# First chunk of a weight load requested as 120 partitions and 8 partitions

## The chip, the cores and the metric

One core of a Trainium2 chip. The metric is the device time of one execution in microseconds (us). The profile's span is about 1.9 us shorter than that time (80.7 us of span in a run of 82.61 us), and all instants below are counted from the start of the span. Engines: PE is TensorE, PEld its weight loader, DVE VectorE, ACT ScalarE, SP the sync engine that issues nearly all transfers.

## The reference, cut to what matters

A decoding step for one token: layer norm, grouped attention over a window of 4096 cached positions (8 K and V heads, 32 query heads), and beside it a gated feed-forward block; both results are added to the input.

```python
xn = layernorm(x)
out = x + attention(xn, k_cache, v_cache, wq) @ wo + (xn + (silu(xn @ w_gate) * (xn @ w_up)) @ w_down * sigmoid(xn @ w_r))
```

With one row of input there is next to no reuse: each byte of 30.67 MB is read once, and the kernel is a stream of loads with the arithmetic laid beside it. The end of the stream is `wo` (4096 x 512, bf16, 4 MB) and `w_down` (1792 x 512, 1.75 MB).

## The kernel before

Every transfer has its own semaphore. SP issues the whole stream in one order: wq, K cache, V cache, w_gate, w_up, wo in four chunks, w_down in five.

```python
def dma(eng, name, out_, in_):
    s = S("d_" + name)
    eng.dma_start(out=out_, in_=in_).then_inc(s, 16)
    return (s, 16)
...
wo_chunks = [(0, 8), (8, 16), (16, 24), (24, 32)]          # of 32 blocks of 512 columns
t_wo = [dma(sy, f"wo{k}", wo_sb[:, j0 * D:j1 * D], wo_v[:, j0 * D:j1 * D]) for k, (j0, j1) in enumerate(wo_chunks)]
wd_v = B_w_down.rearrange("(p j) n -> p (j n)", j=FB)      # 128 partitions x 14 blocks
wd_chunks = [(0, 4), (4, 8), (8, 11), (11, 13), (13, 14)]
t_wd = [dma(sy, f"wd{k}", wd_sb[:, j0 * D:j1 * D], wd_v[:, j0 * D:j1 * D]) for k, (j0, j1) in enumerate(wd_chunks)]
```

A chunk of wo is 1 MB (8 KB a partition), the first of w_down 512 KB (4 KB a partition). PE takes the chunks in the same order and adds everything up in one PSUM row:

```python
for k, (j0, j1) in enumerate(wo_chunks):
    PE.need(t_wo[k])
    for j in range(j0, j1):
        te.matmul(a_ps, lhsT=oT2[:, j:j + 1], rhs=wo_sb[:, j * D:(j + 1) * D], ...)
PE.need(t_hT)
for k, (j0, j1) in enumerate(wd_chunks):
    PE.need(t_wd[k])
    for j in range(j0, j1):
        ins = te.matmul(a_ps, lhsT=hTr[:, j, 0:1], rhs=wd_sb[:, j * D:(j + 1) * D], ...)
```

Then one DVE addition and the store of 1 KB.

## Time and profile before

| | before |
|---|---|
| time, median (range) | 82.52 us (82.39 to 82.57, 3 runs) |
| span of the profiled run | 80.7 us |
| last landing mark of wo / of w_down | 72.80 / 77.28 us |
| end of the last matmul | 77.81 us |

A *landing mark* is one DMA engine's increment of a transfer's semaphore, as the trace records it. A transfer of 128 rows has sixteen marks in the trace, one for each of the 16 engines, and the sixteenth is what PE waits for: wo's last is at 72.80 us, PE's next matmul starts at 72.84.

### The profile page before, as it was taken

What the parts mean: (1) busy time and instruction counts of PE and PEld (TensorE: products, weight loads), DVE (VectorE), ACT (ScalarE), POOL (GpSimd) and SP (SyncE); (2) the same over time, 40 slices, a digit from 0 to 9 for tenths busy, and PEclk for the clock granted to TensorE, in tenths of its full rate; (3) what the DMA queues carried; (4) which work ended last, traced back from release to release, by engine and by line L of the source; (5) the groups of instructions that cost most, each with busy time, mean ns of one, the idle gap of its engine ahead of it and who ended that gap; (6) DMA issues with size and microseconds to landing.
All of it is one profiled execution on the core that took longest, in us unless ns stands there. A gap on an engine that the chain in (4) does not pass through costs nothing.

```text
span 80.7 us, 1552 instructions
## 1 busy us (share of the span) xinstructions
PE 60.5 (75%) x596; PEld 29.9 (37%) x596; DVE 43.5 (54%) x103; ACT 29.7 (37%) x40; POOL 7.3 (9%) x27
## 2 busy tenths in 40 slices
PE   0012945589999999999988968877888887788950
PEld 0012201386657768667732323222233322123300
DVE  3775000195678977968736678888763380000030
ACT  1941001305696896895860422442222200000000
POOL 5910000101112112121200000000000000000000
PEclk9999999555799999999999999999999999999999
DMA  1899998999999999999999999999999999999400
GB/s 33 309 439 390 455 447 374 434 418 434 418 430 410 434 410 430 414 434 406 430 410 430 406 430 414 445 447 412 426 419 413 418 426 418 416 402 398 138 2 1
DMA packets 4185, 30.72 MB, mean 381 GB/s; under 512 B 467, under 2 KB 598, under 8 KB 1110
## 3 DMA queue, kind: packets, MB, share of 16 engines
q1 hardware_dynamic: 4178, 30.67, 91.7%
q8 instruction: 2, 0.03, 0.2%
q14 instruction: 1, 0.01, 0.0%
q10 hardware_dynamic: 4, 0.00, 0.0%
HBM read 30.67 MB, written 0.00 MB: 380 GB/s over the span
## 4 chain that ended last, share of the span: by engine, by line
SPq 48%; DMA 40%; PE 6%; issue 2%; DVE 1%
SPq L151 48%; DMA k_sb<-in_A_wo_dram 40%; PE ps L467 4%; PE ps L462 2%; DVE res L471 1%; SPq L500 0%; SPq L74 0%
## 5 line engine op out<-in xcount | busy, mean ns | idle before, releaser
L276 ACT COPY kT<-ps 128x1024 bf16<-128x1024 bf16 x19 | 18.5, 1019 | 8.8 <-PE ps L302 8.7
L302 PE MATMUL ps<-ident_bf,kin 128*128 128x128 bf16 x256 | 18.7, 231 | 0.8 <-DVE kin L268 0.6
L302 PEld LDWEIGHTS ps<-ident_bf,kin 128*128 128x128 bf16 x256 | 15.8, 104 | 5.1 <-issue 4.2
L268 DVE COPY kin<-k_sb 128x1024 bf16<-128x1024 bf16 x32 | 12.2, 422 | 0.7 <-PE ps L302 0.7
L273 DVE COPY kT<-ps 128x1024 bf16<-128x1024 bf16 x13 | 9.0, 692 | 4.4 <-PE ps L302 4.3
L462 PE MATMUL ps<-k_sb,oT 128*1 128x512 bf16 x32 | 7.5, 378 | 2.0 <-DMA k_sb<-in_A_wo_dram 2.0
L394 ACT CAST pvS<-ps 128x512 bf16<-128x512 f32 x8 | 4.7, 586 | 9.6 <-PE ps L399 9.6
L471 DVE TENSOR_TENSOR res<-ps,resid 1x512 bf16<-1x512 f32 x1 | 0.7, 679 | 11.5 <-PE ps L467 11.5
L375 DVE COPY vin<-v_sb 128x2048 bf16<-128x2048 bf16 x8 | 5.5, 686 | 1.4 <-PE ps L408 1.4
L381 DVE COPY vin<-v_sb 128x2048 bf16<-128x2048 bf16 x8 | 5.5, 683 | 0.0
L408 PE MATMUL ps<-vin,pTcur 128*16 128x512 bf16 x32 | 3.1, 381 | 2.6 <-ACT pvS L394 2.2
L462 PEld LDWEIGHTS ps<-k_sb,oT 128*1 128x1 bf16 x32 | 2.4, 83 | 7.1 <-DMA k_sb<-in_A_wo_dram 3.2
L420 PE MATMUL ps<-zmov,zst 128*128 128x512 bf16 x16 | 4.7, 377 | 0.0
L228 PE MATMUL ps<-wq_sb,xnT 128*1 128x512 bf16 x32 | 2.9, 499 | 2.3 <-DMA wq_sb<-in_A_wq_dram 2.3
L310 PE MATMUL ps<-kT,qB 128*32 128x512 bf16 x36 | 4.2, 413 | 0.4 <-ACT kT L276 0.3
L244 DVE COPY qpad<-ps 128x16 bf16<-128x16 bf16 x2 | 0.3, 174 | 7.6 <-PE ps L240 7.6
L310 PE MATMUL ps<-kT,qA 128*32 128x512 bf16 x32 | 4.4, 417 | 0.0
L259 POOL COPY qA<-qpad 128x32 bf16<-128x32 bf16 x8 | 2.0, 255 | 20.6 <-DVE qpad L244 10.9
L194 PE MATMUL ps<-ident_bf,xn_row 1*128 1x1 bf16 x4 | 0.3, 165 | 4.6 <-DVE xn_row L189 4.6
L147 PE MATMUL ps<-zmov,zst 128*128 128x512 bf16 x14 | 3.7, 382 | 0.0
L234 ACT CAST q<-ps 128x512 bf16<-128x512 f32 x2 | 1.1, 589 | 6.6 <-PE ps L228 6.6
L414 PE MATMUL ps<-vin,pTcur 128*16 128x512 bf16 x32 | 3.1, 382 | 0.2 <-DVE vin L381 0.2
(85 smaller groups left out, 50.2 us busy)
## 6 DMA issues: line engine op xcount, KB each, us to landing
k_sb<-in_A_k_cache_dram SPq DMA_DIRECT2D x8, 1024.0 KB, 20.6
v_sb<-in_A_v_cache_dram SPq DMA_DIRECT2D x8, 1024.0 KB, 28.2
wq_sb<-in_A_wq_dram SPq DMA_DIRECT2D x2, 2048.0 KB, 9.5
k_sb<-in_A_wo_dram SPq DMA_DIRECT2D x4, 1024.0 KB, 32.0
wq_sb<-in_B_w_gate_dram SPq DMA_DIRECT2D x1, 1792.0 KB, 29.3
wq_sb<-in_B_w_up_dram SPq DMA_DIRECT2D x1, 1792.0 KB, 31.4
k_sb<-in_B_w_down_dram SPq DMA_DIRECT2D x2, 512.0 KB, 31.4
k_sb<-in_B_w_down_dram SPq DMA_DIRECT2D x1, 384.0 KB, 25.7
```

The lines of the kernel that those rows point to most:

```text
L147: te.matmul(ps[:, 7, :], lhsT=zst[:], rhs=zmov[:], start=True, stop=True)
L151: eng.dma_start(out=out_, in_=in_).then_inc(s, 16)
L268: ve.tensor_copy(out=kin[:, b, :], in_=k_sb[:, g, b, :]).then_inc(s_c[b], 1)
L273: ve.tensor_copy(out=kT[:, b, :], in_=tp[:, b, :]).then_inc(s_ev[b], 1)
L276: ac.copy(out=kT[:, b, :], in_=tp[:, b, :]).then_inc(s_ev[b], 1)
L302: ins = te.transpose(tp[:, b, k * P:(k + 1) * P], kin[:, b, k * P:(k + 1) * P], ident_bf[:])
L310: ins = te.matmul(sc[32 * cq:32 * cq + 32, ch, :], lhsT=q[:], rhs=kT[:, b, e * 512:(e + 1) * 512], start=False, stop=False, tile_position= ...
L375: ve.tensor_copy(out=vin[:, 0], in_=v_sb[:, g, 0:16, :]).then_inc(s_va, 1)
L381: ve.tensor_copy(out=vin[:, 1], in_=v_sb[:, g, 16:32, :]).then_inc(s_vb, 1)
L394: ac.copy(out=pvS[:].rearrange("p t d -> p (t d)"), in_=pv_ps).then_inc(s_pvs, 1)
L420: te.matmul(ps[:, 7, :], lhsT=zst[:], rhs=zmov[:], start=True, stop=True)
L462: te.matmul(a_ps, lhsT=oT2[:, j:j + 1], rhs=wo_sb[:, j * D:(j + 1) * D], start=False, stop=False, skip_group_check=True)
```

## The change

Its intent, as far as the words of it tell: 15 engines carry the first chunk of w_down, so the sixteenth has 32 KB less, and what lies behind on its ring (the queue of transfers that one engine works through in order, as the latest engine's marks show: 72.80 us for wo's last chunk, then 74.07, 75.36, 76.30, 76.97 and 77.28 for the five of w_down) lands earlier. The remaining 8 partitions are fetched by a small transfer of their own, one row each on eight engines.

```diff
-    t_wd = [dma(sy, f"wd{k}", wd_sb[:, j0 * D:j1 * D], wd_v[:, j0 * D:j1 * D]) for k, (j0, j1) in enumerate(wd_chunks)]
+    t_wd = []
+    for k, (j0, j1) in enumerate(wd_chunks):
+        rows = [(0, 120), (120, P)] if k == 0 else [(0, P)]
+        t_wd.append([dma(sy, f"wd{k}_{p0}", wd_sb[p0:p1, j0 * D:j1 * D], wd_v[p0:p1, j0 * D:j1 * D]) for p0, p1 in rows])
@@
-        PE.need(t_wd[k])
+        PE.need(*t_wd[k])
```

## The prediction

The traces do not number the engines. The numbers in the prediction are names: 15 for the engine that the 120 rows leave out, 0 to 7 for those that carry a row of the small transfer as well, 8 to 14 for the rest. "Crowding" means that engines slow one another by what they write at the same time. A_wo is wo.

> **What bounds the kernel now.** I read the page first, then the chain that ended last in order of time, then the timeline of the tail, then the transfers of the last microseconds, and at the end the record of single landings in the trace. The page has the 16 DMA engines at 9 tenths or full from slice 3 to the last tenth of the span, and the chain says which transfer counts:
>
> ```profile
> DMA  1899998999999999999999999999999999999400
> GB/s 33 309 439 390 455 447 374 434 418 434 418 430 410 434 410 430 414 434 406 430 410 430 406 430 414 445 447 412 426 419 413 418 426 418 416 402 398 138 2 1
> ...
> q8 instruction: 2, 0.03, 0.2%
> ...
> SPq 48%; DMA 40%; PE 6%; issue 2%; DVE 1%
> ```
>
> ```profile
> 40.85 31.95 DMA k_sb<-in_A_wo_dram
> 72.80 0.04 issue
> 72.84 1.89 PE ps L462 x8
> 74.73 3.10 PE ps L467 x14
> 77.83 0.02 issue
> 77.86 0.68 DVE res L471
> ```
>
> So the chain is: the DMA stream up to the landing of the fourth and last chunk of A_wo (72.80 us), then 22 matmuls on PE without a break (8 on that chunk, 14 on w_down), then one addition and the store. No landing of w_down is in it. That is the point of the whole case, because the change touches w_down alone. The timeline seems to contradict it:
>
> ```profile
> 72.84 1.89 PE L462 MATMUL ps<-k_sb,oT 128*1 128x512 bf16 x8 [0.61 <-DMA k_sb<-in_A_wo_dram]
> 74.35 0.73 PEld L467 LDWEIGHTS ps<-k_sb,hTr 128*1 128x1 bf16 x4
> 74.56 3.25 PE L467 MATMUL ps<-k_sb,hTr 128*1 128x512 bf16 x14
> 75.40 0.55 PEld L467 LDWEIGHTS ps<-k_sb,hTr 128*1 128x1 bf16 x4 [0.32 <-DMA k_sb<-in_B_w_down_dram]
> 76.34 0.30 PEld L467 LDWEIGHTS ps<-k_sb,hTr 128*1 128x1 bf16 x3 [0.40 <-DMA k_sb<-in_B_w_down_dram]
> 77.01 0.09 PEld L467 LDWEIGHTS ps<-k_sb,hTr 128*1 128x1 bf16 x2 [0.36 <-DMA k_sb<-in_B_w_down_dram]
> 77.32 0.08 PEld L467 LDWEIGHTS ps<-k_sb,hTr 128*1 128x1 bf16 x1 [0.23 <-DMA k_sb<-in_B_w_down_dram]
> ```
>
> Four weight loads wait for w_down, 0.32 + 0.40 + 0.36 + 0.23 = 1.31 us. But a weight load runs beside the matmul before it, and the PE row shows its 14 matmuls as one group without a gap. What the waits cost must be read from the starts of the matmuls. Undisturbed, one follows another after 0.215 us (eight of them from 72.84 to 74.56). In the trace the steps over the four borders between w_down chunks are 0.215, 0.272, 0.232 and 0.215 us, so the waits cost 0 + 0.057 + 0.017 + 0 = about 0.075 us together. The wait of 1.31 us is an artefact of the weight loader's running ahead.
>
> Next, the transfers of 74 to 80 us, in slices of 0.15 us:
>
> ```profile
> DMA  9999999791111100000000000000000000000000
> GB/s 403 389 362 403 410 348 341 266 280 62 48 41 55 48 27 14 27 27 14 0 0 0 0 0 0 0 0 0 0 0 0 0 0 0 0 7 0 0 0 0
> ```
>
> Up to 75.3 us all engines work (403 GB/s is about 16 times 25), then about two (41 to 62), then one alone (27) till 76.85. So two engines lag. The sixteen landing marks of each transfer in the trace say by how much. Up to the 2nd chunk of the V cache (37.6 to 37.9 us) all sixteen engines land within 0.33 us. From the third chunk on, one is about 0.73 us behind the fourteen others; from the fifth on, another is 1.4 us behind them, and it stays so to the end. For A_wo's last chunk the fourteenth mark is at 71.33, the fifteenth at 72.08, the sixteenth at 72.80 us; for w_down's first 72.62, 73.36, 74.07; for its last 75.86, 76.56, 77.28. Call the engines A (0.7 us late) and B (1.4 us). The packet records show the origin. [...] On B a 16 KB instruction fetch (queue 8) at 44.78 took 1.06 us and the packet after it 0.80. After that both rings simply run late.
>
> [...]
>
> **The change, part by part.** Engine instructions stay as they are, apart from one more transfer issued on SP and one more semaphore for PE to wait for.
>
> 1. *Taken away from engine 15:* its share of w_down's first chunk, 8 rows of 4 KB. In the landings that chunk takes each engine 72.28 to 71.00 = 1.28 us, so 0.16 us a row. Everything behind it on that ring lands 1.28 us earlier.
> 2. *Added to engines 0 to 7:* one row of 4 KB each, +0.16 us for the later chunks on these rings.
> 3. *Added on SP:* one issue. An unblocked one takes about 0.43 us, and all five issues of w_down end at 60.7 us, against a first landing of w_down after 72 us. Cost 0.
> 4. *Added on PE:* a second wait before w_down. The one there now takes 0.05 us at 74.10 and is hidden behind queued matmuls. Cost 0 to 0.05 us.
> 5. *What does not move:* A_wo's last landing at 72.80 us. It stands ahead of w_down on every ring, so removing bytes behind it cannot bring it forward.
>
> If B is engine 15, its last mark falls from 77.28 to 76.00, and A becomes the last: 76.56 us, or 76.72 if it is among engines 0 to 7. The DMA stream then ends 0.56 to 0.72 us earlier. PE, however, starts at 72.84 regardless and has 22 matmuls: the last begins at 72.84 + 21 x 0.215 = 77.355 and ends 0.38 later at about 77.73, where it now ends at 77.81. The gain at the end is the 0.075 us of steps worked out above, 0.1% of 82.52: the change frees over half a microsecond of the stream and PE can use under a tenth of it.
>
> **The rivals.**
> - *B is not engine 15 but among 0 to 7.* Then B carries a row more: the four later chunks land 0.16 us later. Run through the matmul steps, the third chunk starts at 76.50 instead of 76.35 and everything after it moves along: +0.16 us, 82.68. For it: nothing numbers the engines. Against it: the author chose the fifteen-engine form, presumably because engine 15 was late. If B is one of 8 to 14, nothing happens at all.
> - [...] If the first chunk ran at half its rate, it would take up to 1.28 us more on fifteen engines (an estimate from item 1). With B on 15 the last mark would be A's, 76.56 + 1.28 = 77.84 plus perhaps 0.16, and the end up to 0.7 us later (83.2). With B among the others, up to 1.4 us (83.9). Against it: engines are already staggered by 0.3 us and more, so they rarely meet row for row.
> - *The full gain of the stream, 0.6 to 0.7 us (81.8 to 81.9).* This is what one expects who reads the 1.31 us of weight-load waits as lost time. Against it stands the unbroken row of 14 matmuls. It could only come true if A_wo landed earlier as well.
> - *The instruction fetches move.* A fetch of 1.06 us that comes earlier, later, or on another ring in the changed program moves A_wo's landing, and with it the end, by up to about 0.7 us either way (A is the next behind B). Hardly likely from one added instruction on SP.
>
> **Range and chances.** I give 55% to "B is 15, no crowding" (82.4 to 82.5), 25% to a loss of 0.1 to 0.2 us, 15% to crowding with +0.3 to +1.4 us, and 5% to a shift of the fetches. The three runs of before spread over 0.18 us. Middle: 82.5; range 82.2 to 82.9. Two per cent is 1.65 us: no gain of that size is to be had where PE's unbroken row leaves 0.1 us, so faster 1%; the worst crowding reaches 1.7%, so slower 2%; within 2%: 97%.
>
> **What would show it right or wrong.** Right, step by step: the 120-partition piece has fifteen landing marks and the other eight; the last chunk of w_down has its sixteenth mark near 76.0 to 76.8 us instead of 77.28 while A_wo's stays near 72.8; the waits of the weight loads for w_down shrink from 1.31 us or vanish; the steps between the 22 matmuls are 0.215 throughout; the addition starts 0.05 to 0.1 us earlier. Wrong on B's number: the sixteenth mark still some 1.4 us behind, 0.16 later than before. Wrong on crowding: rows of w_down's first chunk that take clearly over 0.16 us. Wrong altogether: a time under 82.1 us, which would mean that A_wo's landing moved or that PE's row was not the bound.

## More of the kernel before

The profile's views of the tail stand in the prediction. One more helps later: stretches of the tail, of which only the last two columns count here, the mean busy share of the 16 DMA engines and what they moved. (The columns ahead of them are the busy times of PE, PEld, DVE, ACT and POOL, and PE's granted clock.)

```profile
71.00:73.60 2.60, 1.99 (x10) 0.67 (x9) 0.00 (x0) 0.00 (x0) 0.00 (x0) 1.00 1.02 406
73.60:76.00 2.40, 2.40 (x13) 0.87 (x11) 0.00 (x0) 0.00 (x0) 0.00 (x0) 1.00 0.76 280
```

Share 1 and 406 GB/s belong together: sixteen busy engines at some 25 GB/s each. When the share falls, the bytes fall with it.

## The result, and the profile after

The changed kernel takes 85.16 us in the median (84.61 to 85.94, 4 runs), before 82.5 (82.39 to 82.57, 4 runs): 3.0% slower, ratio 1.0302 with a 95% interval of 1.0252 to 1.0353. It is outside the predicted range. (Ratios here are the mean time of one kernel's fast runs over that of the other's fast runs of the same rounds, so not quite the ratio of the medians quoted; e7_second120 is an exception, named there. On one core "slow" is a run over 1.5% above the fastest of its kernel; the 85.94 is one.)

The last lines of the chain of waits after, in order of time (start, duration, what):

```profile
43.27 33.69 DMA k_sb<-in_B_w_down_dram
76.95 0.09 issue
77.04 3.40 PE ps L470 x14
80.44 0.02 issue
80.47 0.68 DVE res L474
```

A landing of w_down, at 76.95 us, is now in the chain, where before wo's at 72.80 stood. It is the first chunk, the one that was cut. The timeline of the tail after:

```profile
74.81 1.89 PE L465 MATMUL ps<-k_sb,oT 128*1 128x512 bf16 x8 [2.52 <-DMA k_sb<-in_A_wo_dram]
77.01 0.55 PEld L470 LDWEIGHTS ps<-k_sb,hTr 128*1 128x1 bf16 x4 [0.82 <-issue]
77.04 3.39 PE L470 MATMUL ps<-k_sb,hTr 128*1 128x512 bf16 x14 [0.35 <-DMA k_sb<-in_B_w_down_dram]
78.03 0.52 PEld L470 LDWEIGHTS ps<-k_sb,hTr 128*1 128x1 bf16 x4 [0.48 <-DMA k_sb<-in_B_w_down_dram]
```

PE's wait ahead of wo's last chunk has grown from 0.61 to 2.52 us, although wo was not touched and is issued before w_down. And the stretches of the tail after:

```profile
68.50:71.00 2.50, 1.90 (x10) 0.59 (x8) 0.00 (x0) 0.00 (x0) 0.00 (x0) 1.00 1.00 408
71.00:73.60 2.60, 1.29 (x6) 0.33 (x4) 0.00 (x0) 0.00 (x0) 0.00 (x0) 1.00 1.05 204
73.60:76.00 2.40, 1.19 (x6) 0.50 (x7) 0.00 (x0) 0.00 (x0) 0.00 (x0) 1.00 0.98 237
76.00:78.00 2.00, 1.65 (x8) 0.36 (x5) 0.00 (x0) 0.00 (x0) 0.00 (x0) 1.00 0.84 302
```

From 71.0 us, when the first engines reach the cut chunk, the engines are as busy as ever (1.05 and 0.98) and move half the bytes (204 and 237 GB/s). They are not starved; each packet takes about twice as long or more. The packet records agree: w_down's 4 KB packets took 0.16 us each before (256 of them, medians of each half microsecond 0.159 to 0.165). After, 197 of the 256 took more than 0.21 us, with medians of 0.27 to 0.31 us from 71.0 to 72.5 us and 0.38 to 0.46 from 72.5 to 74.0.

The landing marks of the tail, before and after (fourteenth, fifteenth and sixteenth to land; two increments at 43.88 and 50.23 us, in the transfers of 120 and of 8 rows and long before their data, left out, so that the 120 rows have fifteen marks and the thirteenth stands for the last engine that is not late):

```
                       before                 after
wo, last chunk         71.33  72.08  72.80    71.61  73.94  74.76
w_down, 1st chunk      72.62  73.36  74.07    74.45  75.98  76.95   (120 rows)
                                              74.50         76.33   (8 rows)
w_down, 2nd chunk      73.89  74.64  75.36    76.42  77.42  77.99
w_down, 5th chunk      75.86  76.56  77.28    78.34  79.32  79.89
```

Three things are in these figures. The engines that are not late need 2.85 us for the cut chunk instead of 1.29. On the two late engines wo's last chunk, ahead of the cut one on their rings, lands 1.9 to 2.0 us later than before. And both late engines have marks in the transfer of 120 rows (75.98 and 76.95 us): neither of them is the engine that the change relieves.

### The profile page after: what moved, and what is told of

Its sections match the earlier page's. It is cut to its first block, busy times and chain, and to the rows that moved or that the text cites. A ratio compares the mean times of both kernels' runs of the same rounds, so it can differ in the third digit from the quotient of the medians.

```text
span 83.3 us, 1553 instructions
## 1 busy us (share of the span) xinstructions
PE 61.7 (74%) x596; PEld 30.5 (37%) x596; DVE 43.6 (52%) x103; ACT 29.7 (36%) x40; POOL 7.3 (9%) x27
## 4 chain that ended last, share of the span: by engine, by line
DMA 54%; PE 25%; SPq 11%; DVE 5%; issue 1%
DMA k_sb<-in_B_w_down_dram 40%; DMA wq_sb<-in_A_wq_dram 14%; PE ps L302 13%; SPq L151 11%; PE ps L310 4%; PE ps L470 4%; PE ps L228 2%; DVE kin L268 2%; DVE kT L273 2%; PE ps L240 1%; DVE res L474 1%; DVE qpad L244 0%; SPq L503 0%; SPq L74 0%
## 5 line engine op out<-in xcount | busy, mean ns | idle before, releaser
L228 PE MATMUL ps<-wq_sb,xnT 128*1 128x512 bf16 x32 | 3.8, 621 | 1.8 <-DMA wq_sb<-in_A_wq_dram 1.8
L411 PE MATMUL ps<-vin,pTcur 128*16 128x512 bf16 x32 | 3.1, 381 | 2.6 <-ACT pvS L397 2.2
L470 PE MATMUL ps<-k_sb,hTr 128*1 128x512 bf16 x14 | 3.4, 378 | 0.3 <-DMA k_sb<-in_B_w_down_dram 0.3
```

The source lines that it names most:

```text
L228: ins = te.matmul(ps[32 * c:32 * c + 1, hf, :], lhsT=xnT[:, kt:kt + 1], rhs=wq_sb[:, kt, (4 * hf + c) * 512:(4 * hf + c + 1) * 512], start ...
```

## The experiments

The first eight ran on one chip, on which the kernel before took 82.66 us (82.29 to 82.9, up to 12 runs), the last four on another, on which it took 82.59 (82.33 to 82.77, 11 runs). Each run is compared with the kernel before on its own chip. The theory: what a packet costs depends on which partitions the engines write at the same time (crowding); its figures stand first in the expectations, ahead of the rivals. Rivals: the further transfer or PE's second wait costs; fifteen engines or an odd count cost; the reading side costs; the small transfer costs.

### The disputed cost by itself (e1_micro)

The body of the kernel is replaced by thirteen loads from the K cache, one after another, each of 32 KB a row. Its output is wrong, which doesn't matter for the time. It was executed once (100.78 us).

```diff
+    def layout(name, n, step):
+        dst = bass.AP(k_sb, 0, [[step * row, n], [4096, 4], [1, 4096]])   # n partitions, `step` apart
+        SP.need(dma(sy, name, dst, src[0:n]))
+    layout("r128s1", 128, 1)
+    layout("r120s1", 120, 1)
+    ...
+    layout("r8s1", 8, 1)
+    layout("r8s4", 8, 4)
+    layout("r8s16", 8, 16)
+    ...
```

> Measures the disputed cost by itself (the result is wrong on purpose: x is stored). Thirteen transfers, each of 32 KB a row in four packets of 8 KB, one after the other; only the number of rows and the step between the partitions differ. An uncrowded packet took 0.309 us in the kernel before. [...] 128 rows 0.31 us a packet; 120 and 64 rows about 0.62 [...]; 16 rows in a run about 1.24, 16 rows at step 4 about 0.62; 8 rows in a run about 1.24, 8 rows at step 4 about 0.31, at step 16 about 0.62; 11 rows in a run about 1.2, at step 12 about 0.31; 4 rows in a run 1.24, at step 32 0.62; one row 0.31. Rival (the reading side, or the number of engines, is what costs): the packet time depends on the number of rows alone, the same at every step, so 8 rows at steps 1, 4 and 16 agree. Rival (only the odd count of 120 is bad): 64 rows take 0.31.

| rows, step | median packet of 8 KB, us | first packet to last landing mark, us | expected packet, us |
|---|---|---|---|
| 128, 1 | 0.309 | 11.33 (32 packets an engine) | 0.31 |
| 120, 1 | 0.647 | 21.08 (32) | 0.62 |
| 64, 1 | 0.639 | 10.94 (16) | 0.62 |
| 16, 1 | 1.162 | 5.38 (4) | 1.24 |
| 16, 4 | 0.492 | 3.08 (4) | 0.62 |
| 8, 1 | 1.044 | 5.20 (4) | 1.24 |
| 8, 4 | 0.309 | 1.65 (4) | 0.31 |
| 8, 16 | 0.439 | 2.96 (4) | 0.62 |
| 11, 1 | 0.954 | 5.19 (4) | 1.2 |
| 11, 12 | 0.380 | 2.10 (4) | 0.31 |
| 4, 1 | 0.859 | 5.16 (4) | 1.24 |
| 4, 32 | 0.393 | 2.80 (4) | 0.62 |

The loads of 8 rows decide it. They read the same bytes of HBM, use the same number of engines, and differ only in the partitions written; they take 1.65, 2.96 or 5.20 us. With 0.4 us from the last packet to the last mark, four packets of 0.309 us make 1.64; twice that time a packet, 2.87; four times, 5.34. (In the short crowded loads the medians of a packet lie under what was expected, for instance 0.439 instead of 0.62. There the first packets are as short as 0.31, and 0.8 to 1.65 us pass between the last packet and the last mark, so the time to the last mark is the safer measure.) The stretches of the profile say it in bandwidth. In order: 128 rows; 120 rows; 8 rows at step 1; 8 rows at step 4 (the columns are POOL's busy time, PE's clock, the DMA share and GB/s):

```profile
3.30:14.20 10.90, 0.00 (x0) 1.00 0.93 384
15.70:36.20 20.50, 0.00 (x0) 1.00 0.91 190
...
61.00:66.20 5.20, 0.00 (x0) 1.00 0.33 46
67.80:69.10 1.30, 0.00 (x0) 1.00 0.44 183
```

So the reading side and the number of engines are out, and so is the odd count, for 64 rows suffer as 120 do. The thirteenth load, of one row, missed its expected 0.31 us: it went to four engines (four marks), all on one partition, and its packets took 0.437 us.

How rows are dealt to the engines, and what it is that engines share when they crowd, no run shows. Of the 480 packets of the load of 120 rows, 405 took 0.60 to 0.70 us, and all fifteen marks lie between 36.20 and 36.74 us. An engine that crowded with no other would, by an estimate (32 packets of 0.309 us make 9.9, against the 21.08 measured), have finished some 10 us before the others; none did. So the factor of two is measured for all fifteen engines, and why it is two stays open. One case missed what was expected: 11 rows at step 12 took 2.10 us, where 8 rows at step 4, with the same 0.31 us expected for a packet, took 1.65. That one stays unexplained too.

### Which engines are late (e2_probe)

```diff
+    t_probe = [dma(sy, f"pr{r}", wq_flat[0:r, 14336 + 128 * r:14464 + 128 * r], wd_v[0:r, 0:128]) for r in range(1, 16)]
```

(At the end POOL waits for these transfers as well.)

> The kernel before with fifteen tiny transfers of 1 to 15 rows behind the last chunk of w_down, to number the two late engines by their landing marks: [...] If instead B is one of 8 to 14, as the 120-row transfer of the changed kernel suggests (it has two late marks), a second mark 1.4 us late appears from some row count between 9 and 15 on. Time: within 0.5 us of before; the tiny transfers end before the store.

The run took 82.37 us. Each further row adds one engine and so one mark; an engine's marks in successive probes are some 0.18 us apart. The marks that a probe added were ordinary ones, at 75.8 to 76.2 us, with two exceptions. The probe of 4 rows added one at 76.96 us, which is 0.21 us behind A's mark in w_down's last chunk (76.74). The probe of 12 rows added one at 77.37, 0.18 us behind B's (77.19). So A is the engine that the fourth row adds, and B the one that the twelfth adds; no other of the fifteen was late in this run. In the changed kernel both late engines have marks in the transfer of 120 rows, so the change relieved neither.

### The parts of the change in place

Controls and parts, each on the changed kernel's loop over the rows (the lines below are cut to what differs). First the same number of transfers and waits without crowding (e6_cols2), then a crowded split that leaves the bytes of each engine as they were (e5_half64):

```diff
-        rows = [(0, 120), (120, P)] if k == 0 else [(0, P)]
+        cols = [(0, 2), (2, 4)] if k == 0 else [(j0, j1)]        # e6_cols2: all 128 partitions, half of each row
+        rows = [(0, 64), (64, P)] if k == 0 else [(0, P)]        # e5_half64
```

> Control: first chunk of w_down as two transfers of all 128 partitions, 2 KB of each row apiece. As many transfers and waits as the changed kernel, no crowding. [...] as before, 82.4 to 82.7 us. Rival (the further transfer, its issue, or PE's second wait costs): 83 us and up.

82.66 us (82.58 to 82.86), ratio 1.0012 (0.9978 to 1.0046). A further transfer, its issue and PE's further wait cost nothing that can be seen. Its chain of waits is that of the kernel before:

```profile
72.80 0.04 issue
72.85 1.89 PE ps L465 x8
74.73 3.17 PE ps L470 x14
```

> First chunk of w_down as rows 0 to 63 and rows 64 to 127: both use all 16 engines, four rows each, the bytes of each engine are as before. [...] 0.31 us a row instead of 0.16, the chunk lasts 2.5 us instead of 1.28, and the two late engines are slowed in A_wo's last chunk as in the changed kernel: about 84 to 85 us. Rival (leaving an engine out, 15 engines, or the unbalanced bytes cost): 82.5 us.

86.1 us (85.8 to 86.32), ratio 1.0418 (1.0380 to 1.0457): more than expected, and more than the changed kernel. Sixteen engines with equal bytes (in e1_micro 64 rows, 256 packets, made sixteen packets an engine) lose as much as fifteen, so neither leaving an engine out nor the imbalance is the cause. In this profile wo's last mark is at 74.81 us and w_down's at 79.86, nearly the same as in the changed kernel, yet the last matmul ends a microsecond later. The trace says why: TensorE's granted clock, the share of its full clock that the trace records, is one half from 76.14 to 79.56 us, and in that time the matmuls follow one another after 0.427 us instead of 0.215. I had not foreseen that, and come back to it.

Next the split without its small transfer (e3_only120), and the split moved to the second and to the last chunk:

```diff
-        rows = [(0, 120), (120, P)] if k == 0 else [(0, P)]
+        rows = [(0, 120)] if k == 0 else [(0, P)]                # e3_only120, wrong result on purpose
+        rows = [(0, 120), (120, P)] if k == 1 else [(0, P)]      # e7_second120
+        rows = [(0, 120), (120, P)] if k == 4 else [(0, P)]      # e8_last120
```

> The changed kernel without the transfer of 8 rows (rows 120 to 127 of the first chunk keep other data, so the result is wrong on purpose). [...] the 120 rows alone still take about 0.31 us a row, so most of the loss stays: about 84.4 to 84.8 us, with 0.3 to 0.8 us less than the changed kernel for the eight rows [...]. Rival (the small transfer is the cause): back to 82.5 us.

85.83 us (84.96 to 86.06), ratio 1.0388 (1.0354 to 1.0421). The 120 rows alone carry the loss; the saving that I expected from leaving out eight rows did not show. The profiled run was the fastest of five (84.96) and the one with a mean clock of 1.00.

> The split of 120 and 8 rows moved from the first chunk of w_down to the second, of the same size. By then the late engines have 0.1 to 0.3 us of A_wo left at most. If the loss has two parts, the lengthened chunk (about 1.3 to 1.6 us of the stream) and the delay of A_wo's last landing on the late engines, the second part vanishes: A_wo lands at 72.8 to 73.0 us in the profile, and the time is about 83.8 to 84.3 us. If the stream's lengthening alone is the loss: about 85.1 us as in the changed kernel.

86.15 us (84.78 to 87.32, two of four runs slow by the rule above), ratio 1.0429 (1.0360 to 1.0497). In the profile wo's last mark is back at 73.15 us, near what was expected, but the time is not lower. The recorded ratio comes out only with the two slow runs counted in (mean of all four 86.10 us). The two fast ones, 84.78 and 85.57, have a mean of 85.18, which is 3.1% over 82.6 and what was expected if the stream's lengthening alone is the loss. With two fast runs and a spread of 2.5 us over all four, this decides nothing yet about the two parts.

> The split moved to the last chunk of w_down, with rows of 1 KB, a quarter of the first chunk. Crowding in proportion to bytes: a chunk of 0.33 us becomes 0.65 and the eight rows cost 0.1 to 0.2 more, so 82.8 to 83.1 us. If the cost is a fixed one for each transfer of 120 rows: 85 us.

82.81 us (82.67 to 83.05), ratio 1.0019 (0.9985 to 1.0053). The loss is no fixed price of a transfer of 120 rows. That it goes in proportion to the bytes of the crowded chunk is not shown: a quarter of 2.6 us would be 0.65, and the interval reaches to 0.44 only.

### PE's unbroken row (e4_wosplit)

```diff
-    wo_chunks = [(0, 8), (8, 16), (16, 24), (24, 32)]
+    wo_chunks = [(0, 8), (8, 16), (16, 24), (24, 28), (28, 32)]
```

> The kernel before with the last chunk of A_wo cut into two of four rows each; nothing else. It tests the step of the prediction that PE's unbroken row of 22 matmuls leaves under 0.1 us. If so: 0.05 to 0.12 us faster (82.4 us), because PE then starts the row about 1.2 us earlier and ends 0.4 us after the last landing. If another transfer costs by itself: slower by up to 0.3 us.

82.64 us (82.47 to 82.8), ratio 0.9999 (0.9973 to 1.0026). No gain can be seen. The interval is too wide for 0.1%, and the lateness of the latest engine varies by more than that: wo's last mark lies at 72.69 to 73.00 us in the profiles whose tail is not crowded. So the 0.075 us of the prediction is not contradicted, nor is it shown; what is shown is that nothing large was to be had there.

### The clock, and the same cuts without it (e9 to e12)

Half clock in the tail would blur every comparison above, so after one more measurement of the changed kernel (e9_again) the last three runs take it out: idle matmuls keep PE busy in its long wait.

```diff
     for k, (j0, j1) in enumerate(wo_chunks):
+        if k == 3:
+            fill(5)          # ten matmuls, 2.15 us; fill(2) in e12_second120fill
         PE.need(t_wo[k])
```

> The changed kernel once more, on one chip with the next three. [...] 84.6 to 86.0 us as at first, a spread of over 1 us, because in some executions TensorE's clock is halved for one window of 3.41 us after its wait of 2.5 us for A_wo's last chunk, in others not.

> The changed kernel with ten idle matmuls (2.15 us) ahead of PE's wait for A_wo's last chunk, so that PE is busy in the wait and still ready when the chunk lands at 74.7 us. If the halved clock makes the spread: all runs at 84.6 to 85.2 us, spread under 0.6 us, matmul steps of 0.215 us to the end. Rival (the spread comes from the transfers): the same median and spread as the changed kernel.

The changed kernel again: 85.96 us (85.74 to 86.07, 5 runs), ratio 1.0400 (1.0379 to 1.0421). With the filling: 84.80 us (84.37 to 85.27, 6 runs), ratio 1.0272 (1.0239 to 1.0305). The timeline of PE, first without and then with the filling:

```profile
74.73 3.25 PE L465 MATMUL ps<-k_sb,oT 128*1 128x512 bf16 x8 [2.52 <-DMA k_sb<-in_A_wo_dram]
77.77 3.55 PE L470 MATMUL ps<-k_sb,hTr 128*1 128x512 bf16 x14
```

```profile
71.99 2.33 PE L147 MATMUL ps<-zmov,zst 128*128 128x512 bf16 x10
74.41 1.89 PE L467 MATMUL ps<-k_sb,oT 128*1 128x512 bf16 x8
76.59 3.41 PE L472 MATMUL ps<-k_sb,hTr 128*1 128x512 bf16 x14 [0.29 <-issue]
```

Eight matmuls take 3.25 us without and 1.89 with it. In the first run the trace shows a granted clock of one half from 75.10 to 78.51 us, a window of 3.41 us behind a wait of 2.52; in the second, none in the tail. The same wait of 2.52 us had brought no half clock in the first profile of the changed kernel, whose granted clock is 1.00 from 66.0 to 80.5 us.

The clock records offer a reason, an estimate of mine. All their stretches but the last of each are whole multiples of 3.413 us long (3.413, 6.827 and 61.44 us in the kernel before), so that, if a border lies at every multiple, windows of 3.413 us can be laid through each profile. In e9_again the wait fell into one window (71.69 to 75.10 us, of which PE was busy 0.89), and the next one ran at half clock; so it was in e5_half64 (72.73 to 76.14, busy 1.29). In the first profile of the changed kernel a border at 73.98 us cut the wait in two (busy 1.73 and 2.24 us), in e3_only120 one at 73.97 (1.61 and 2.45), and the clock stayed full. How little work is too little cannot be read from this: in e11_only120fill a window with 1.68 us of work, ahead of the tail, was followed by half clock.

The medians differ by 1.16 us, and in the two profiles most of the difference is the clock: w_down's last mark is at 79.66 and 79.46 us, the end of the last matmul at 81.33 and 80.00. Both expected spreads were missed. The changed kernel spread over 0.33 us, not over 1, with a mean clock under 1 in all five runs; with the filling it spread over 0.90, not under 0.6, and six runs of it had mean clocks of 0.96 to 1.00 without a relation to their times. So the filling took away a loss here and not a spread. What spreads the filled runs was not tested.

> As the run before, without the transfer of 8 rows (wrong result on purpose). Earlier the profiles of the two forms ended within 0.25 us. If the eight rows cost little: 84.4 to 85.0 us, 0.1 to 0.4 us under the run with them. If the eight rows were much of the loss: under 84 us.

84.77 us (84.35 to 85.03), ratio 1.0262 (1.0234 to 1.0291): 0.03 us below the run with the eight rows. The small transfer costs nothing that can be seen at the end, although its rows crowd too (8 neighbouring rows took 5.20 us in e1_micro, 8 rows at step 4 took 1.65).

> The split on the second chunk of w_down, with four idle matmuls ahead of the same wait. A_wo lands at 73.0 to 73.3 us. If the delay of A_wo's last landing is a part of its own of the loss: 84.2 to 84.8 us, 0.3 to 0.7 us under the run with the split on the first chunk. If only the stream's lengthening counts: the same time as that run.

85.21 us (84.65 to 86.42, one of six slow), ratio 1.0307 (1.0275 to 1.0339): not below e10_fill but, if anything, above. (The spans of the two, without what lies outside the profile, have the same median, 83.05 us; why some runs of this kernel take up to 1.2 us more outside the span than others, no trace shows.) My theory of two separate losses, a longer stream and a late wo, falls. The chain of this run's tail shows the reason:

```profile
43.70 33.76 DMA k_sb<-in_B_w_down_dram
77.45 0.04 issue
77.50 2.43 PE ps L472 x10
```

wo's last mark is at 73.28 us instead of 74.36, as intended. But now the second chunk lands at 77.46 with ten matmuls behind it, where in e10_fill the first lands at 76.50 with fourteen behind it: 77.46 + 10 x 0.215 and 76.50 + 14 x 0.215 are within 0.1 us of each other. What counts is by how much the crowded chunk lengthens the ring that lands last, and that is the same: w_down's last mark is at 79.38 and 79.46 us. So the delay of wo is not an addition to that lengthening; it is a part of it, seen earlier on the ring.

No version that beats the kernel before came out of this. To relieve A and B alone one would have to choose the engines, and the 120 rows tried here left out another one, at the price of crowding. Other ways were not tried.

## Why the prediction was wrong, point by point

- *What bounds the kernel before, the two late engines and how late they are*: right; the later profiles show two late engines too, with lags of 0.6 to 1.0 and 1.1 to 1.6 us ahead of the crowded part. By the order in time the lags of the kernel before began with two packets of the kind that the page lists as instruction, one of 8 KB on queue 14 at 37.50 us (0.34 us, the packet after it 0.97 instead of 0.31) and one of 16 KB on queue 8 at 44.78 us (1.06 us, the packet after it 0.80). The fifteen and eight landing marks of the two transfers came as expected. That the weight loader's waits are no lost time was not contradicted, but e4_wosplit could not resolve 0.1 us.
- *Item 1 (what leaves engine 15) and the case "B is engine 15", given 55%*: wrong. One mark of the second chunk, by its lead that of the engine that the 120 rows leave out, did come earlier (74.27 us, the next one 75.81). But it is not a late engine: both of those have marks among the 120 rows (75.98 and 76.95 us), and the probe puts them at the fourth and the twelfth row. I had taken the author's choice of fifteen engines as a hint; it did not hold here. By the prediction's own reckoning this alone would have cost the expected gain of 0.075 us and no more.
- *Item 2 (one more row on engines 0 to 7, +0.16 us)*: too small for A, where the mark of the eight rows lies 0.35 us behind that of the 120. At the end it made no difference that could be seen (e11_only120fill).
- *Items 3 and 4 (issue, second wait)*: right, 0 to within the interval of e6_cols2 (-0.2 to +0.4 us).
- *The rival of crowding*: this is the cause, and here is the step that failed. I sized it at up to 1.28 us on the stream, said "engines are already staggered by 0.3 us and more, so they rarely meet row for row", and gave it 15%; the worst end it allowed was 83.9 us. Its own sign came true: rows of the cut chunk took 0.27 to 0.46 us instead of 0.16. Measured: the punctual engines need 2.85 instead of 1.29 us for the cut chunk (+1.56) and another 0.70 us more for the eight rows and the second chunk; the stream ends 2.61 us later (77.28 to 79.89). A stagger of 0.3 us is no protection, because the crowding is not a chance meeting: in the 120-row load of e1_micro the packets start at 0.3 to 0.4 us and then stay near 0.65, on all fifteen engines, to the end. (What keeps all fifteen so, no run shows.)
- *Item 5 ("what does not move: A_wo's last landing at 72.80 us")*: wrong, 74.76 us. I argued from the order on a ring. But the late engines were still writing wo when the others began with the cut chunk, and their 8 KB packets of wo then took 0.40 to 0.82 us instead of 0.31: the order on a ring held, but its packets were slowed by what other engines wrote. On the latest engine (B) the account is +1.96 us until wo has landed, +0.92 for the first chunk of w_down (2.19 instead of 1.27), and -0.27 for the rest, together 2.61.
- *What PE makes of it*: the method of the matmul steps holds. The last matmul ends 2.63 us later (77.81 to 80.44), the span grows by 2.6.
- *Not in the prediction at all*: the clock. PE's new wait of 2.5 us is followed by a half-clock window in some profiles (75.10 to 78.51 us in e9_again) and not in others (the first of the changed kernel). In the two profiles it makes up most of the difference between e9_again and e10_fill, whose medians are 1.16 us apart. It belongs to what the changed kernel costs, but it follows from the crowding and is no second root. Without it the change still costs 2.7% (e10_fill).

What stays open, beside how 120 rows are dealt, is why the crowded chunk takes 2.2 times as long in the kernel and not exactly twice. That the late engines' packets of wo (0.40 to 0.82 us then, instead of 0.31) and the early engines' packets of the next chunk crowded with it is a guess of mine; it was not tried.

## What to carry to other kernels

What a transfer cost here depended on which partitions its engines wrote at the same time: 64 and 120 partitions moved at half the rate of 128 (203 and 190 GB/s against 384), eight rows at a third of their rate when they lay side by side instead of four apart (5.20 us against 1.65), and the crowded transfer also slowed what other engines were still writing (packets of wo took 0.40 to 0.82 us instead of 0.31). To cut a transfer, try to cut its columns and keep all 128 partitions (82.66 us in e6_cols2, as before). Before shaping a transfer to relieve a late DMA engine, find that engine with a few transfers of 1 to 15 rows; and read the DMA share together with GB/s, for here a share of 1.05 at 204 GB/s, half the bandwidth, meant crowding, not speed.
